# Loading two tokens per partition in 512-byte packets for the first chunk of a retention + GELU kernel, with its A, y and S products on smaller TensorE tiles

One core of one Trainium2 chip. The metric is the device time of one execution in microseconds (us); smaller is better. Runs are told fast or slow by their time and granted clock; only fast runs are compared: ratios are of fast runs alone, while medians are of all four runs of a kernel and say where one of them was slow.

## The reference, cut to what matters

```python
# q, k, v: [4 batches, 8 heads, 768 tokens, 64], float32
gamma = 1 - 2 ** (-5 - arange(8))                    # a decay per head
for t in range(768):
    state = gamma * state + einsum('bhd,bhe->bhde', k[:, :, t], v[:, :, t])
    y[:, :, t] = 1/8 * einsum('bhd,bhde->bhe', q[:, :, t], state)
x = y as rows [3072, 512]                            # token rows, heads side by side
out = gelu_tanh(x @ w_in) @ w_out                    # w_in [512, 2048], w_out [2048, 512]
```

The kernel works in six chunks of 128 tokens. Within a chunk it forms A = k qᵀ per head, multiplies by a decay mask, takes y = vᵀ A plus the part from the state, and updates the state with S = kᵀ v. Then come the two dense products. Chunk 0 has no state yet, so it needs q, k and v of its 128 tokens only, and it is the one chunk with nothing else to hide behind.

## The kernel before

Loads of chunk 0. A tile holds one token per partition, all 8 heads side by side; a head's token is 64 floats, so every packet has 256 bytes. One transfer per tile, over 128 partitions:

```python
def load1(eng, nm, c, b):
    eng.dma_start(out=ld_tile(nm, c, b),             # [128, 8, 64] float32
                  in_=srcs[nm][b, :, c*C:(c+1)*C, :].rearrange("h p d -> p h d"))
...
load1(nc.scalar, "q", 0, 0); load1(nc.sync, "k", 0, 0); load1(nc.scalar, "k", 0, 1)   # ... 12 tiles
```

A and y of a pair of heads, and the rows that leave:

```python
for hp in range(4):
    for j in range(2):                               # A: 64 rows x 128 columns, K = 64
        nc.tensor.matmul(out=ps[j][:, hp], lhsT=t[j*64:(j+1)*64, 1, hp], rhs=t[j*64:(j+1)*64, 0, hp], ...)
...
rows = out[b*S + c*C : b*S + (c+1)*C, :]             # 128 rows of 2048 bytes, one transfer
```

The order of GpSimd (POOL) in the opening; it issues the w_in and w_out loads, with a cast from float32, and prepares k:

```python
prep1(PO, "k", 0, 1)
nc.gpsimd.tensor_copy(out=misc[0:1, 4:5], in_=ld_tile("k", 0, 2)[0:1, 0, 0:1])   # waits for k of batch 2
load_w_in(0); load_w_in(1)
prep1(PO, "k", 0, 2); prep1(PO, "k", 0, 3)
for i in range(2, 5): load_w_in(i)
for i in range(4): load_w_out(i)
```

In program order TensorE takes for each batch the transposes of q and k, A, y; between them `spin(n)`, n dummy matmuls that are meant to keep its clock up. Then the first w_in products on half the tokens, S of each batch, the other half. After that the full 512-column products of w_in begin with "fc 4".

## Time and profile before

| | before |
|---|---|
| time, median (lowest to highest), 4 runs | 212.49 us (211.91 to 213.19) |
| span of the profiled execution | 210.3 us |
| TensorE (PE) busy, granted clock | 97%, 0.997 |
| start of fc 4 on the TensorE timeline (called F) | 21.03 us |
| from F to the end | 189.2 us |
| loads of chunk 0: transfers, rate from 4 to 11 us | 12, 288 GB/s |
| last load issued / first w_in issued / first w_in packet | 7.61 / 8.73 / 13.16 us |

(The prediction takes F from the chain of waits, which gives 21.19 to the same event.) F comes from one execution; the fast executions of the kernel before have spans from 210.2 to 212.8 us, so a difference in F of less than about 1 us is not read.

```profile
64.34 1.40 SPq L642 DMA_DIRECT2D out_dram<-o_sb  x3
65.79 4.28 SPq L98 DMA_DIRECT2D v<-in_v_dram  x4
```

In the first, w_in is issued and k of batches 2 and 3 prepared right after. In the second, three output tiles of chunk 0 leave on the SP queue in 1.4 us of issue, and the loads of v for chunk 2 follow without delay.

### The profile page before, as it was taken

To read this page: it belongs to the slowest core of one execution; us is meant where nothing else is said; L and a number is where in the kernel's file an instruction comes from. 1 tells how busy PE (TensorE), PEld (TensorE's weight loads), DVE (VectorE), ACT (ScalarE), POOL (GpSimd) and SP (SyncE) were. 2 spreads that over 40 slices of the span, in tenths; PEclk is the share of its full clock that TensorE was granted. 3 is DMA by queue.
4 is the path that set the end of the run, shared out by engine and by line. 5 is a ranking of instruction groups with operands and counts; after the bars stand their busy time and mean duration, and the time that the engine had idled before them with its cause. 6 is when DMAs were issued, how large, how long until landed. Compare 5 with 4: busy or idle time off the path is not lost.

```text
span 210.3 us, 3858 instructions
## 1 busy us (share of the span) xinstructions
PE 203.5 (97%) x1502; PEld 110.3 (52%) x1502; DVE 91.4 (43%) x162; ACT 84.3 (40%) x141; POOL 100.0 (48%) x121
## 2 busy tenths in 40 slices
PE   7789999999999999999999999999999999999993
PEld 2448444457897456444465444456444455444462
DVE  6678100298634757351847522647550652100001
ACT  2465661245465122565113566113466113565120
POOL 3596400433366867663787939651697611100000
PEclk9999999999999999999999999999999999999998
DMA  7999999997879989969988889897897021100112
GB/s 158 288 251 206 207 203 224 225 248 135 148 109 233 243 175 226 179 107 183 237 146 225 167 155 253 165 198 161 161 242 171 10 94 50 53 0 0 50 71 79
DMA packets 132738, 33.83 MB, mean 161 GB/s; under 512 B 126512, under 2 KB 130864, under 8 KB 132720
## 3 DMA queue, kind: packets, MB, share of 16 engines
q1 hardware_dynamic: 117328, 21.80, 53.3%
q0 software_dynamic: 5600, 8.65, 17.4%
q10 hardware_dynamic: 9792, 3.15, 6.2%
q8 instruction: 11, 0.18, 0.3%
q14 instruction: 7, 0.06, 0.1%
HBM read 31.48 MB, written 6.29 MB: 180 GB/s over the span
## 4 chain that ended last, share of the span: by engine, by line
PE 92%; DMA 3%; POOL 1%; ACT 1%; SPq 1%; DVE 0%; issue 0%
PE o_ps L469 40%; PE h_ps L424 40%; PE y_ps L299 3%; DMA k<-in_k_dram 3%; PE a_ps L264 3%; PE y_ps L286 2%; PE s_ps L318 2%; PE qkT_ps L239 1%; POOL w_in L408 1%; PE spin_ps L171 1%; POOL k L195 1%; SPq L98 1%; ACT qkT L224 0%; ACT v L190 0%; DVE o_sb L507 0%
## 5 line engine op out<-in xcount | busy, mean ns | idle before, releaser
L469 PE MATMUL o_ps<-w_out,g 128*128 128x512 f16 (+1 forms) x400 | 88.6, 371 | 0.0
L424 PE MATMUL h_ps<-xT,w_in 128*128 128x512 f16 (+1 forms) x464 | 85.6, 342 | 0.0
L439 ACT ACTIVATE g<-h_ps 128x512 f16<-128x512 f32 x96 | 57.3, 597 | 46.9 <-PE h_ps L424 46.8
L424 PEld LDWEIGHTS <-w_in 128*128 128x128 f16 x464 | 44.8, 98 | 37.4
L469 PEld LDWEIGHTS <-g 128*128 128x128 f16 x400 | 37.4, 98 | 38.6
L277 DVE TENSOR_TENSOR a_sb<-a_ps,mask 128x512 f16<-128x512 f32 x48 | 30.2, 684 | 17.9 <-PE a_ps L264 17.8
L491 ACT COPY o_sb<-o_ps 128x512 f32<-128x512 f32 x19 | 11.1, 586 | 51.5 <-PE o_ps L469 49.7
L195 POOL TENSOR_TENSOR k<-k,cst 128x512 f16<-128x512 f32 x23 | 23.9, 1061 | 12.5 <-DMA k<-in_k_dram 12.4
L344 POOL TENSOR_TENSOR stg<-st,cst 128x512 f32<-128x512 f16 x16 | 16.4, 1039 | 12.6 <-DVE st L335 10.7
L206 POOL TENSOR_TENSOR kT<-kT,cst 128x512 f16<-128x512 f32 x16 | 16.3, 1050 | 10.7 <-DMA kT<-in_k_dram 10.2
L496 POOL DMA_DIRECT2D out_dram<-o_sb x17 | 9.5, 562 | 23.0 <-ACT o_sb L491 16.1
L254 DVE STREAM_TRANSPOSE qkT<-q 128x512 f16<-128x512 f16 x16 | 11.4, 712 | 13.8 <-POOL q L206 13.8
L206 POOL TENSOR_TENSOR q<-q,cst 128x512 f16<-128x512 f32 x16 | 16.3, 1050 | 1.8 <-PE h_ps L424 1.8
L254 DVE STREAM_TRANSPOSE qkT<-kT 128x512 f16<-128x512 f16 x16 | 10.9, 698 | 13.3 <-POOL kT L206 13.3
L335 DVE TENSOR_TENSOR st<-s_ps,stg 64x256 f16<-64x256 f32 x32 | 13.5, 422 | 5.0 <-PE s_ps L318 4.4
L195 DVE TENSOR_TENSOR q<-q,cst 128x512 f16<-128x512 f32 x8 | 6.1, 757 | 16.5 <-DMA q<-in_q_dram 16.5
L226 DVE CAST xT<-y_ps 128x512 f16<-128x512 f32 x11 | 7.2, 687 | 12.7 <-PE y_ps L299 12.7
L192 POOL CAST v<-v 128x512 f16<-128x512 f32 x16 | 9.6, 616 | 6.3 <-DMA v<-in_v_dram 5.2
L507 DVE COPY o_sb<-o_ps 128x256 f32<-128x256 f32 x2 | 0.8, 424 | 26.6 <-PE o_ps L469 26.6
L224 ACT CAST xT<-y_ps 128x512 f16<-128x512 f32 x13 | 7.2, 587 | 11.8 <-PE y_ps L299 11.8
L171 PE MATMUL spin_ps<-zero 128*128 128x512 f16 x30 | 8.9, 437 | 1.3 <-DVE zero L139 1.3
L264 PE MATMUL a_ps<-qkT 64*128 64x128 f16 x192 | 8.1, 218 | 1.3 <-ACT qkT L224 1.3
(34 smaller groups left out, 88.2 us busy)
## 6 DMA issues: line engine op xcount, KB each, us to landing
v<-in_v_dram SPq DMA_DIRECT2D x22, 256.0 KB, 4.3
k<-in_k_dram SPq DMA_DIRECT2D x20, 256.0 KB, 4.4
out_dram<-o_sb POOLq DMA_DIRECT2D x17, 256.0 KB, 3.0
q<-in_q_dram SPq DMA_DIRECT2D x64, 64.0 KB, 2.8
kT<-in_k_dram SPq DMA_DIRECT2D x64, 64.0 KB, 2.8
w_out<-in_moe_w_out_dram POOLq DMA_DIRECT2D x4, 512.0 KB, 16.1
w_in<-in_moe_w_in_dram POOLq DMA_DIRECT2D x3, 512.0 KB, 9.4
q<-in_q_dram SPq DMA_DIRECT2D x5, 256.0 KB, 5.9
```

The lines of the kernel that those rows point to most:

```text
L171: nc.tensor.matmul(out=ps, lhsT=zero[:, 0:128], rhs=zero, start=True, stop=True)
L195: eng.tensor_tensor(out=t, in0=src, in1=cst[:, col:col + H].unsqueeze(2).broadcast_to([128, H, Dh]), op=ALU.mult,)
L206: nc.gpsimd.tensor_tensor(out=t, in0=ld_all((key, c))[:, b * NHP:(b + 1) * NHP].rearrange("p hp a d -> p (hp a) d"), in1=cst[:, col:col + ...
L254: nc.vector.transpose(out=qkT_tile(c, b)[:, "qk".index(nm)].rearrange("p hp t -> p (hp t)"), in_=blk16.pop((nm, c, b)).rearrange("p ha d - ...
L264: nc.tensor.matmul(out=ps[j][:, hp], lhsT=t[j * 64:(j + 1) * 64, 1, hp], rhs=t[j * 64:(j + 1) * 64, 0, hp], start=True, stop=True,)
L277: nc.vector.tensor_tensor(out=s, in0=ps[j], in1=mask[:, j], op=ALU.mult)
L335: eng.tensor_tensor(out=st[sl, :, b, sl], in0=s_ps[sl, :, sl], in1=stg[sl, :, b, sl], op=ALU.add,)
L344: nc.gpsimd.tensor_tensor(out=stg[:, :, b], in0=st[:, :, b], in1=cst[:, OG:OG + NHP].unsqueeze(2).broadcast_to([128, NHP, 128]), op=ALU.mult,)
L424: nc.tensor.matmul(out=out, lhsT=w_in_of(fc, kc), rhs=xT[c][:, kc, t0:t1], start=(kc == 0 and first), stop=(kc == NHP - 1), skip_group_che ...
L439: nc.scalar.activation(out=out, in_=in_, func=AF.Gelu_apprx_tanh, scale=1.0)
L469: nc.tensor.matmul(out=ps[:, n0:n1], lhsT=g_sb[c, fc // 2][:, fc % 2, b * C:(b + 1) * C], rhs=w_out_sb[fc // (NF // NO)][:, fc % (NF // NO ...
L491: nc.scalar.copy(out=o_sb, in_=ps)
```

## The change

Its intent: 512-byte packets for the loads of chunk 0, as the DMA engines are full there with 256-byte ones. A partition takes tokens 2t and 2t+1 of a head; heads 0 to 3 lie on partitions 0 to 63, heads 4 to 7 on 64 to 127. Hence two transfers of 64 partitions per tile, 64x64 tiles for A and y, 64-row tiles for S, masks for permuted tokens, and permuted output rows. The order of work in chunk 0 was changed with it. The core of the diff:

```diff
+    def load_pair(eng, nm, b):
+        for hh in range(2):
+            eng.dma_start(
+                out=ld_tile(nm, 0, b)[hh*64:(hh+1)*64].rearrange("p (mi e) d -> p mi (e d)", e=2),
+                in_=srcs[nm][b, hh*4:(hh+1)*4, 0:C, :].rearrange("mi (tp e) d -> tp mi (e d)", e=2))
     def load1(eng, nm, c, b):
+        if c == 0:
+            load_pair(eng, nm, b)
+            return
# ... masks: eight memsets and one select become six selects on 64 partitions; the old mask is made later
     def mm_A(c, b):
+        if c == 0:
+            for n in range(16):
+                m, e, i, hh = n >> 3, n >> 2 & 1, n >> 1 & 1, n & 1
+                nc.tensor.matmul(out=ps[i][hh*64:(hh+1)*64, 2*m+e],
+                                 lhsT=t[i*64:(i+1)*64, 1, 2*hh+m, e*64:(e+1)*64],
+                                 rhs=t[i*64:(i+1)*64, 0, 2*hh+m], ...)
# ... likewise y (16 matmuls, two banks) and S (8 per batch on two row tiles, two banks, four copies)
     def ev_O(c, b):
         rows = out[b*S + c*C : b*S + (c+1)*C, :]
+        if c == 0:
+            rows = rows.rearrange("(t e) n -> e t n", e=2)
# ... order in chunk 0, POOL:
     prep1(PO, "k", 0, 1)
     (wait for k of batch 2)
     load_w_in(0)
+    prep1(PO, "k", 0, 2)
     load_w_in(1)
-    prep1(PO, "k", 0, 2)
     prep1(PO, "k", 0, 3)
# ... v of batch 2 loaded by SP instead of ACT; first qkT copy on DVE instead of ACT; y before the next A; 18 spins in place of 16 after the first 14 (cut)
```

More of the change, by code (lines that the diff above doesn't have):

```diff
@@ L50 @@
     kdec_t = g_t ** (160.0 - t_t)
-    cst_np = np.concatenate([qdec, kdec, gst, qdec_t, kdec_t], axis=1).astype(np.float32)
+    hh_p, tp_p = np.arange(128)[:, None] // 64, np.arange(128)[:, None] % 64
+    mi_c, e_c = np.arange(8)[None, :] // 2, np.arange(8)[None, :] % 2
+    g_p, t_p2 = gam[4 * hh_p + mi_c], 2.0 * tp_p + e_c
+    qdec_p = g_p ** (t_p2 - 32.0) * 0.125
+    kdec_p = g_p ** (160.0 - t_p2)
+    ig_p = 1.0 / g128[4 * hh_p + np.arange(8)[None, :] // 2 % 2 * 2 + np.arange(8)[None, :] // 4]
+    ig = np.tile(1.0 / np.concatenate([g128[0::2], g128[1::2]]), (128, 1))
+    cst_np = np.concatenate(
+        [qdec, kdec, gst, qdec_t, kdec_t, qdec_p, kdec_p, ig_p, ig], axis=1
+    ).astype(np.float32)
     cst_h = nc.inline_tensor(cst_np, name="rr_cst")
@@ L64 @@
     OQ, OK, OG, OQT, OKT = 0, H, 2 * H, 2 * H + NHP, 2 * H + NHP + 16
+    OQP, OKP, OIP, OI, NCST = OKT + 16, OKT + 24, OKT + 32, OKT + 40, OKT + 48
     misc = const.tile([128, 32], F32)
-    cst = const.tile([128, 64], F32)
+    cst = const.tile([128, 128], F32)
     iden = const.tile([128, 128], F16)
@@ L95, in ld_tile @@
         return raw[nm, c, b]
+    def load_pair(eng, nm, b):
+        for hh in range(2):
+            eng.dma_start(
+                out=ld_tile(nm, 0, b)[hh * 64:(hh + 1) * 64].rearrange(
+                    "p (mi e) d -> p mi (e d)", e=2
+                ),
+                in_=srcs[nm][b, hh * 4:(hh + 1) * 4, 0:C, :].rearrange(
+                    "mi (tp e) d -> tp mi (e d)", e=2
+                ),
+            )
     def load1(eng, nm, c, b):
+        if c == 0:
+            load_pair(eng, nm, b)
+            return
         eng.dma_start(
@@ L124, in hold @@
         nc.gpsimd.tensor_copy(out=ld_tile(nm, c, b)[0:1, 0, 0:1], in_=until)
-    nc.sync.dma_start(out=cst[:, :OKT + 16], in_=cst_h.ap())
+    nc.sync.dma_start(out=cst[:, :NCST], in_=cst_h.ap())
     load1(nc.scalar, "q", 0, 0)
@@ L134 @@
     load1(nc.sync, "q", 0, 3)
+    load1(nc.sync, "v", 0, 2)
     load1(nc.sync, "v", 0, 3)
@@ L139 @@
     nc.vector.memset(zero, 0.0)
-    mask = const.tile([128, 2, NHP, 128], F32, name="mask")
     nc.vector.memset(iden, 1.0)
-    for j in range(2):
-        for hp in range(NHP):
-            nc.vector.memset(mask[:, j, hp], float(1.0 / g128[2 * hp + j]))
     nc.gpsimd.affine_select(
@@ L154, with make_mask @@
     )
-    nc.gpsimd.affine_select(
-        out=mask.rearrange("p j hp t -> p (j hp) t"),
-        in_=mask.rearrange("p j hp t -> p (j hp) t"),
-        pattern=[[0, 2 * NHP], [1, 128]],
-        base=0,
-        channel_multiplier=-1,
-        compare_op=ALU.is_ge,
-        fill=0.0,
-    )
+    mask_p = const.tile([128, 2, 4, 128], F32, name="mask_p")
+    for hh in range(2):
+        sl = slice(hh * 64, (hh + 1) * 64)
+        for f, e0, de in ((1, 0, 1), (0, 0, 2), (0, 1, 2)):
+            n = 8 // de
+            nc.gpsimd.affine_select(
+                out=mask_p[sl].rearrange("p i s (f t) -> p (i s) f t", f=2)[:, e0::de, f],
+                in_=cst[sl, OIP + e0:OIP + 8:de].unsqueeze(2).broadcast_to([64, n, 64]),
+                pattern=[[0, n], [1, 64]],
+                base=-e0,
+                channel_multiplier=-1,
+                compare_op=ALU.is_ge,
+                fill=0.0,
+            )
+    mask = const.tile([128, 2, NHP, 128], F32, name="mask")
+    def make_mask():
+        nc.gpsimd.affine_select(
+            out=mask.rearrange("p j hp t -> p (j hp) t"),
+            in_=cst[:, OI:OI + H].unsqueeze(2).broadcast_to([128, H, 128]),
+            pattern=[[0, H], [1, 128]],
+            base=0,
+            channel_multiplier=-1,
+            compare_op=ALU.is_ge,
+            fill=0.0,
+        )
     nc.scalar.activation(
@@ L193, in prep1 @@
         else:
-            col = OQ if nm == "q" else OK
+            col = (OQP, OKP, OQ, OK)[(nm == "k") + 2 * (c > 0)]
+            if c == 0:
+                dst = t.rearrange("p (e mi) d -> p mi e d", e=2)
+                src = src.rearrange("p (mi e) d -> p mi e d", e=2)
+                dec = cst[:, col:col + H].rearrange("p (mi e) -> p mi e", e=2)
+                dec = dec.unsqueeze(3).broadcast_to([128, 4, 2, Dh])
+            else:
+                dst, dec = t, cst[:, col:col + H].unsqueeze(2).broadcast_to([128, H, Dh])
             eng.tensor_tensor(
-                out=t,
+                out=dst,
                 in0=src,
-                in1=cst[:, col:col + H].unsqueeze(2).broadcast_to([128, H, Dh]),
+                in1=dec,
                 op=ALU.mult,
@@ L236, in mm_T @@
         ps = bank("att", F16, (128, 2, NHP, 128), "qkT_ps")
-        for i, nm in enumerate("qk"):
+        for i, nm in enumerate("qk") if c == 0 else ():
+            src = h16[nm, c, b].rearrange("p (e m i) d -> p m e (i d)", m=2, e=2)
+            dst = ps[:, i].rearrange("p (hh m) (e t) -> p m e hh t", m=2, e=2)
+            for m in range(2):
+                for e in range(2):
+                    nc.tensor.transpose(out=dst[:, m, e], in_=src[:, m, e], identity=iden)
+        for i, nm in enumerate("qk") if c > 0 else ():
             for hp in range(NHP):
@@ L261, in mm_A @@
         ps = [bank("att", name=f"a_ps{j}") for j in range(2)]
+        pss["A", c, b] = ps
+        if c == 0:
+            for n in range(16):
+                m, e, i, hh = n >> 3, n >> 2 & 1, n >> 1 & 1, n & 1
+                nc.tensor.matmul(
+                    out=ps[i][hh * 64:(hh + 1) * 64, 2 * m + e],
+                    lhsT=t[i * 64:(i + 1) * 64, 1, 2 * hh + m, e * 64:(e + 1) * 64],
+                    rhs=t[i * 64:(i + 1) * 64, 0, 2 * hh + m],
+                    start=True,
+                    stop=True,
+                    skip_group_check=True,
+                )
+            return
         for hp in range(NHP):
@@ L270, in mm_A @@
                 )
-        pss["A", c, b] = ps
     def ev_A(c, b):
@@ L276, in ev_A @@
             s = att.tile([128, NHP, 128], F16, tag=f"a{j}", name=f"a_sb{j}")
-            nc.vector.tensor_tensor(out=s, in0=ps[j], in1=mask[:, j], op=ALU.mult)
+            nc.vector.tensor_tensor(out=s, in0=ps[j], in1=(mask if c else mask_p)[:, j], op=ALU.mult)
             a_sb[c, b, j] = s
     def mm_yc(c, b, tag):
+        if c == 0:
+            pss["Y", c, b] = [bank(tag, name=f"y_ps{hh}") for hh in range(2)]
+            return
         y_ps = pss["Y", c, b] = bank(tag, name="y_ps")
-        if c == 0:
-            return
         for hp in range(NHP):
@@ L296, in mm_yi @@
         y_ps = pss["Y", c, b]
+        for n in range(16) if c == 0 else ():
+            m, e, i, hh = n >> 3, n >> 2 & 1, n >> 1 & 1, n & 1
+            sl = slice(hh * 64, (hh + 1) * 64)
+            nc.tensor.matmul(
+                out=y_ps[hh][i * 64:(i + 1) * 64, m],
+                lhsT=h16["v", c, b][sl, 4 * m + 2 * i + e],
+                rhs=a_sb[c, b, i][sl, 2 * m + e],
+                start=(e == 0),
+                stop=(e == 1),
+                skip_group_check=True,
+            )
+        if c == 0:
+            return
         for hp in range(NHP):
@@ L302, in mm_yi @@
                     rhs=a_sb[c, b, j][:, hp],
-                    start=(c == 0),
+                    start=False,
                     stop=True,
@@ L310, in ev_Y @@
             xT[c] = xp.tile([128, NHP, B * C], F16, tag="x", name="xT")
-        copy_on(eng, xT[c][:, :, b * C:(b + 1) * C], pss.pop(("Y", c, b)))
+        y_ps = pss.pop(("Y", c, b))
+        if c == 0:
+            for hh in range(2):
+                copy_on(
+                    eng[hh] if isinstance(eng, tuple) else eng,
+                    xT[c][:, 2 * hh:2 * hh + 2, b * C:(b + 1) * C],
+                    y_ps[hh][:, 0:2],
+                )
+            return
+        copy_on(eng, xT[c][:, :, b * C:(b + 1) * C], y_ps)
     def mm_s(c, b, tag="att"):
         if c + 1 >= NCk:
+            return
+        if c == 0:
+            s_ps = pss["S", c, b] = [bank(tag, name=f"s_ps{hh}") for hh in range(2)]
+            k_ = h16["k", c, b].rearrange("p (e m i) d -> p m e (i d)", m=2, e=2)
+            v_ = h16["v", c, b].rearrange("p (m i e) d -> p m e i d", m=2, e=2)
+            for n in range(8):
+                m, e, hh = n >> 2, n >> 1 & 1, n & 1
+                sl = slice(hh * 64, (hh + 1) * 64)
+                nc.tensor.matmul(
+                    out=s_ps[hh][:, m],
+                    lhsT=k_[sl, m, e],
+                    rhs=v_[sl, m, e],
+                    start=(e == 0),
+                    stop=(e == 1),
+                    skip_group_check=True,
+                )
             return
@@ L332, in ev_S @@
             if c == 0:
-                copy_on(eng, st[sl, :, b, sl], s_ps[sl, :, sl])
+                for hh in range(2):
+                    copy_on(
+                        eng, st[sl, 2 * hh:2 * hh + 2, b, sl], s_ps[hh][sl, 0:2, sl]
+                    )
             else:
@@ L487, in ev_O @@
         o_sb = op.tile([128, d_model], F32, tag="o", name="o_sb")
+        if c == 0:
+            rows = rows.rearrange("(t e) n -> e t n", e=2)
         if b == B - 1 and c > 0:
@@ L525 @@
     mm_T(0, 0)
-    ev_T(0, 0, AC)
-    load1(AC, "v", 0, 2)
     prep1(VE, "q", 0, 1)
+    ev_T(0, 0)
+    prep1(AC, "v", 0, 0)
     prep1(PO, "k", 0, 1)
@@ L540 @@
         load_w_out(i)
+    make_mask()
     spin(4)
@@ L545 @@
     ev_T(0, 1, AC)
-    prep1(AC, "v", 0, 0)
     prep1(VE, "q", 0, 2)
     spin(3)
-    mm_A(0, 1)
-    ev_A(0, 1)
     mm_yc(0, 0, "o")
@@ L553 @@
     ev_Y(0, 0, AC)
+    mm_A(0, 1)
+    ev_A(0, 1)
+    mm_T(0, 2)
+    ev_T(0, 2, AC)
     prep1(AC, "v", 0, 1)
-    mm_T(0, 2)
-    ev_T(0, 2)
-    spin(3)
+    prep1(VE, "q", 0, 3)
+    spin(5)
     mm_yc(0, 1, "o")
@@ L561 @@
     mm_A(0, 2)
-    prep1(VE, "q", 0, 3)
     ev_A(0, 2)
-    spin(2)
     mm_T(0, 3)
     ev_T(0, 3, AC)
+    prep1(AC, "v", 0, 2)
+    prep1(AC, "v", 0, 3)
     spin(4)
@@ L569 @@
     ev_A(0, 3)
-    prep1(AC, "v", 0, 2)
-    prep1(AC, "v", 0, 3)
+    spin(2)
+    t01, t23 = (0, half), (half, 2 * half)
+    m1a = [moe1_parts(0, fp, *t01) for fp in range(2)]
+    m1a[0](range(2))
+    m1a[1](range(2))
     mm_yc(0, 2, "o")
@@ L574 @@
     ev_Y(0, 2, AC)
-    t01, t23 = (0, half), (half, 2 * half)
-    m1a = [moe1_parts(0, fp, *t01) for fp in range(2)]
-    m1a[0](range(2))
-    mm_s(0, 0)
-    m1a[1](range(2))
+    m1a[0](range(2, 4))
+    m1a[1](range(2, 4))
     mm_yc(0, 3, "o")
@@ L584 @@
     ev_Y(0, 3)
-    m1a[0](range(2, 4))
+    mm_s(0, 0)
+    ev_S(0, 0)
     mm_s(0, 1)
-    m1a[1](range(2, 4))
+    ev_S(0, 1)
     for b in range(2):
-        ev_S(0, b)
         moe1_two(0, b, *t23, "oh"[b])
-        mm_s(0, 2 + b)
+    mm_s(0, 2)
     ev_S(0, 2)
+    mm_s(0, 3)
     ev_S(0, 3)
```

## The prediction

> **What bounds the kernel now.** I read the page first, then the chain that ended last in order of time, then the timeline of the first 22 us. Engine shares come first:
>
> ```profile
> PE 203.5 (97%) x1502; PEld 110.3 (52%) x1502; DVE 91.4 (43%) x162; ACT 84.3 (40%) x141; POOL 100.0 (48%) x121
> PE 92%; DMA 3%; POOL 1%; ACT 1%; SPq 1%; DVE 0%; issue 0%
> ```
>
> TensorE is 97% busy and 92% of the last chain. The change touches chunk 0 of six only, so I ask where in the span the chain is not TensorE. From the chain in order of time:
>
> ```profile
> 2.36 6.18 DMA k<-in_k_dram
> 8.78 1.60 POOL w_in L408 x2
> 10.38 1.08 POOL k L195
> ...
> 14.25 1.01 ACT qkT L224
> 15.26 0.53 ACT v L190
> 15.84 0.41 PE y_ps L299 x8
> ...
> 20.97 0.22 PE s_ps L318 x4
> 21.19 10.36 PE h_ps L424 x48
> 31.55 9.50 PE o_ps L469 x44
> ```
>
> Until 15.8 us the chain runs through loads, POOL, ACT; from there it is TensorE without a gap, and from 21.19 us (the first full 512-column product of w_in, "fc 4") TensorE has the same work in both kernels to the end at about 207 us. So the change is worth what it does to **the moment at which fc 4 starts**; I call it F, and F = 21.19 us now. The loads of that opening:
>
> ```profile
> 4.00:6.00 2.00, 2.00 (x13) 0.95 (x12) 1.38 (x2) 0.57 (x2) 0.00 (x0) 1.00 1.27 287
> 10.00:12.00 2.00, 1.46 (x26) 0.90 (x21) 1.67 (x4) 1.40 (x3) 2.00 (x3) 1.00 1.28 289
> 16.00:18.00 2.00, 2.00 (x31) 1.51 (x28) 1.20 (x3) 0.88 (x2) 1.63 (x3) 1.00 1.26 210
> ```
>
> In these stretches (columns: PE, PEld, DVE, ACT, POOL busy, clock, DMA share, GB/s) the DMA engines are full. 12 tiles of 256 KB land 0.9 us apart at 288 GB/s, q of batch 0 at 3.99 us, v of batch 3 at 14.4; then w_in follows. In the landings behind the timeline, the w_in part that fc 4 needs is complete at 20.07, only 1.1 us before F. Last, the steps of one batch:
>
> ```profile
> 6.88 0.78 DVE L195 TENSOR_TENSOR q<-q,cst 128x512 f16<-128x512 f32 x1 [1.04 <-DMA q<-in_q_dram]
> 8.28 1.29 DVE L277 TENSOR_TENSOR a_sb<-a_ps,mask 128x512 f16<-128x512 f32 x2 [0.62 <-PE a_ps L264]
> 8.76 1.01 ACT L224 COPY qkT<-qkT_ps 128x1024 f16<-128x1024 f16 x1 [1.04 <-PE qkT_ps L239]
> 15.32 0.40 PE L264 MATMUL a_ps<-qkT 64*128 64x128 f16 x8 [0.24 <-ACT qkT L224]
> 17.84 0.69 DVE L226 CAST xT<-y_ps 128x512 f16<-128x512 f32 x1 [0.80 <-PE y_ps L299]
> 18.45 3.66 DVE L226 CAST st<-s_ps 64x256 f16<-64x256 f32 x8
> ```
>
> Per batch: prepare q and k, transpose, copy (about 1 us on ACT, 0.69 on DVE), A, mask (1.29), y, copy (0.59 ACT, 0.69 DVE). These latencies, not the size of the matmuls, are the opening.
>
> **What the Trainium skill says.** (1) "DMA: Bandwidth & Descriptors", section "Why small descriptors are slow (HBM only)": a fixed overhead of about 3 cycles per packet. The trace agrees: dividing 16 engines by packet counts in full stretches, an engine starts a packet every 9.6 ns at 128 B, 14.1 at 256 B, 78.4 at 2048 B: 5 ns plus 36 ns per KB. (2) "SBUF — State Buffer", section "Door 1": a transfer to partitions 0 to 63 reaches 8 of 16 ports and was measured there at 196 GB/s. (3) The same page, "Can I just issue two DMAs to hit both halves?": two transfers to the two halves gained only 6%. No load of the kernel before goes to 64 partitions, so its trace neither confirms nor denies (2) and (3). (4) "TensorEngine Tiling (Array Packing)", "Key Properties": different tiles run in parallel, and a mode switch drains. The trace agrees on the first: the eight A matmuls start in pairs 3 ns apart, a pair every 56 ns.
>
> **The change part by part.**
> *Loads.* 512-byte packets: from the line above 5 + 18 = 23.2 ns, 353 GB/s, a tile in 0.74 us instead of 0.91 (estimate), all twelve 1.97 us sooner. That would move the w_in landing from 20.07 to 18.1: a floor for F, so the whole change can gain at most **3.1 us (1.5%)**. But each tile is now two DMAs of 64 partitions. Both queues begin with the lower half; while both write the same half I expect some 217 GB/s (8 ports at 27.2, the skill's figure), in opposite halves up to 353. Half and half gives 2/(1/217 + 1/353) = 269 GB/s, no better than 288. I take a rate about as before to 20% better: q of batch 1 (fourth tile, 6.85 us before) at 6.2 to 7.0.
> *TensorE.* A and y take 16 matmuls in place of 8, four in parallel: 4 groups x 56 ns + 220 ns = 0.4 us, as before. S takes 8 on two row tiles: as before. Zero, plus perhaps 0.1 us for drains.
> *Evictions.* y is split over two banks: by a fit of 587 ns at 512 and 1010 ns at 1024 columns ACT needs 0.38 us per half, 0.77 for 0.59: +0.18 per batch. DVE (687 ns at 512, 424 at 256): 0.85 for 0.69. S: four 64x128 copies a batch at about 0.29 us, 1.17 for 0.84; mm_s of batch 3 now needs the two banks that S of batch 1 holds.
> *Masks.* Eight DVE memsets (1.15 us) go, but DVE then waits for q at 4.0 us: free. POOL gets six selects on 64 partitions, 2048 columns a partition in place of 1024: some 2.4 us, behind the constants that land at 2.8, so k of batch 1 is prepared from about 5.4, as its load lands. The later mask (1.1 us of POOL after the w_out issues) is beside other work.
> *Order.* The copy of the first transposes goes from ACT (1.01) to DVE (0.69), but behind the preparation of q of batch 1, so it waits for that landing.
>
> Sum, with 353 GB/s: q1 lands 6.2, prepared 7.0, qkT 7.7 (7.72 before), A 8.15, masked 9.55 (9.57 before). y of batch 0 10.0, its copy on ACT to 10.8; transposes of batch 2 copied by ACT 10.85 to 11.85 (0.8 earlier than before, as k2 is prepared between the two w_in issues); v1 on ACT to 12.5; y1 12.95; its copy to 13.8; qkT of batch 3 13.8 to 14.8 (15.26 before). A3 at 14.85, **0.47 sooner**. Then, in TensorE's order: A 0.23, two spins 0.43, w_in products 0.87, y2 0.34, products 0.87, y3 0.4: 18.0. DVE copies y3 to 18.9, S0 to 20.1, S1 to 21.25; TensorE runs the two pairs of w_in products 18.95 to 20.7 and S2, then waits for S1's banks: S3 ends and **F = 21.5**. Before, from A3 to F took 5.87 us; now 6.65: two spins ahead of the products, 0.4 for the wait for y3, 0.3 for S banks. The gain at A3 is given back. At 269 GB/s, q1 lands at 7.0 and all of it comes 0.8 later: F = 22.3. Weighing both, F = 21.5 to 21.9, or +0.3 to +0.7 us.
>
> **The rivals.** *A: the loads dominate and the port limit does not bite.* For it: DMA full from 3 to 34 us, and the chain's 6.18 us in a load of k. Against it: the chain above is held after 8 us by ACT and DVE in turn. If the packets ran at 420 GB/s (the best 2048-byte stretch in the trace was 418), q1 lands 0.6 sooner, F = 20.9, and 212.4 us; with shorter drains and copies than I count, F = 19.5, 211 us.
> *B: the half-partition loads are slower than before.* For it: the skill's 196 GB/s and both queues starting in the same half. At 217 throughout, 12 tiles take 14.5 us instead of 10.9; q3 would land 3 us late at 15, and F = 24: 215.5 us. Against it: two queues, which drift apart.
> *C: a new wait on software-queue loads.* The first packet of w_in came at 13.16, 4.4 us after its issue, just as the ACT queue ran dry. With v2 moved off that queue it runs dry sooner, and w_in mixes with q3, v2 and v3. They could land late; they have 1 to 3 us of slack. Worth within 0.5 us either way.
>
> **Range and chances.** Before is 212.75. My sum gives +0.3 to +0.7; that the order and the spins were visibly re-tuned for this version argues for rival A, so I put the centre at +0.1: 212.9. A at its best and B half-way give 211.0 to 214.8. Faster by 2% needs F at 16.9, below the floor of 18.1 that w_in sets: 0.02. Slower by 2% needs B in full: 0.04. Within 2%: 0.94.
>
> **What would show it.** Right: packets of 512 B in the DMA view; GB/s of 270 to 350 in the opening; A and y groups of 16 in about 0.4 us; fc 4 starting at 21 to 22 us; DVE's S copies or the copy of y3 as what ends TensorE's waits just before it; everything after it unchanged. Wrong: over 380 GB/s, or under 230, in the opening; A groups at 0.6 us; w_in landing as what releases fc 4; or a difference that arises after 25 us.

## More of the kernel before

POOL's timeline (start us, duration us, engine, line, operation), and that of the SP queue, which issues most loads:

```profile
8.73 1.65 POOL L408 DMA_DIRECT2D w_in<-in_moe_w_in_dram  x2
10.38 2.07 POOL L195 TENSOR_TENSOR k<-k,cst 128x512 f16<-128x512 f32 x2
```

## The result

| | before | changed |
|---|---|---|
| time, median (lowest to highest), 4 runs each | 212.49 us (211.91 to 213.19) | 234.37 us (232.59 to 237.43; one run slow) |
| span, granted clock | 210.3 us, 0.997 | 230.9 us, 0.96 |
| F | 21.03 us | 29.43 us (+8.4) |
| from F to the end | 189.2 us | 201.4 us (+12.2) |

The ratio of fast runs is 1.100, 95% interval 1.0915 to 1.1086. (A ratio is the mean time of one kernel's fast runs over that of the other's of the same rounds, so not quite the ratio of the medians.) The prediction, 211.0 to 214.8, was far out. The loss has two parts, 8.4 us before F and 12.2 us after, where nothing was expected.

The page of the changed kernel, engine shares, and shares of the last chain:

```profile
PE 211.5 (92%) x1584; PEld 112.6 (49%) x1584; DVE 90.7 (39%) x163; ACT 84.2 (36%) x144; POOL 102.8 (45%) x127
...
PE 78%; DMA 10%; SPq 7%; POOL 2%; ACTq 1%; DVE 0%; ACT 0%; issue 0%; POOLq 0%
```

TensorE's share of the chain fell from 92% to 78%, and the SP queue, 1% before, has 7%. The chain in order of time (start us, duration us, what) tells where:

```profile
10.55 7.08 DMA k<-in_k_dram
...
17.78 1.04 POOL k L247
...
29.50 10.47 PE h_ps L538 x48
...
75.36 2.00 SPq L760
77.41 4.97 SPq L126
82.44 4.98 SPq L126
87.52 3.11 SPq L126
```

**Before F.** The second half of k of batch 3 took 7.08 us from issue to landing, and everything waited. POOL's timeline (in brackets: idle before, and what ended it):

```profile
10.20 1.03 POOL L247 TENSOR_TENSOR k<-k,cst 128x512 f16<-128x512 f32 x1 [0.39 <-DMA k<-in_k_dram]
...
17.78 1.03 POOL L247 TENSOR_TENSOR k<-k,cst 128x512 f16<-128x512 f32 x1 [5.81 <-DMA k<-in_k_dram]
18.77 2.30 POOL L522 DMA_DIRECT2D w_in<-in_moe_w_in_dram  x3
```

POOL waits for that k until 17.78, and as its queue is in order, the rest of w_in is issued at 18.77 in place of 12.37. What TensorE waited for is k:

```profile
18.87 0.61 PE L295 MATMUL qkT_ps<-iden,k 128*128 128x128 f16 x4 [1.88 <-POOL k L247]
```

It did not wait for w_in afterwards: the third part, the last that fc 4 needs, landed at 24.17 us, 5.3 us before F. From 16 to 18 us TensorE was busy for 0.44 us only, and its clock was then low. The stretches view (PE, PEld, DVE, ACT, POOL busy, clock, DMA share, GB/s):

```profile
18.00:20.00 2.00, 1.13 (x6) 0.71 (x7) 0.00 (x0) 0.48 (x1) 2.00 (x3) 0.50 0.26 69
20.00:22.00 2.00, 2.00 (x20) 0.68 (x19) 0.20 (x1) 1.57 (x3) 2.00 (x4) 0.50 0.61 98
```

The granted clock is 0.50 here (from 17.95 to 24.78 us); in the same stretches of the kernel before it was 1.00. From 18 to 20 us the DMA share is 0.26 too, where full stretches of these kernels read 1.14 to 1.28.

So the 8.4 us are made up as follows. A of batch 3 starts at 21.12 us in place of 15.32: 5.8. From there to F takes 8.31 us in place of 5.71, without a wait of TensorE: with the new order and tiles it is 6.65 at full clock (e1 and e12 below), so 0.9 is theirs, and the other 1.7 goes with the low clock.

**After F.** The SP queue's timeline:

```profile
72.31 5.06 SPq L760 DMA_DIRECT2D out_dram<-o_sb  x3
77.41 14.12 SPq L126 DMA_DIRECT2D v<-in_v_dram  x4
```

Set beside 64.34 and 65.79 of the kernel before: the issue of the same four loads of v takes 14.1 us, not 4.3. The DMA view from 76 to 92 us (40 slices of 0.4 us; busy tenths, then GB/s):

```profile
DMA  1211111111111111128981111111114795111159
GB/s 31 61 41 51 51 51 51 51 51 51 46 51 51 51 51 51 51 77 211 276 205 60 51 51 51 51 51 51 51 51 137 196 297 147 52 46 36 36 127 218
```

For most of that time about a tenth of the engines' time is used, at 51 GB/s. The trace's landing events say which transfers these are: an ordinary transfer raises its semaphore 16 times; each of the three output transfers of chunk 0 on this queue has 3 events, one 0.4 us after its issue ends, and the last at 80.5, 85.6 and 90.7 us: one every 5.1 us, 256 KB / 5.1 us = 51 GB/s. They run two engines wide. The Trainium skill explains it in a place that the prediction did not use: "DMA: Bandwidth & Descriptors", section "Why a DMA increments its semaphore by 16 and not by 1": the number of engines is the largest one up to 16 that divides the slowest dimension (not of size 1) of both sides, and the sequencer adds the missing increments itself. The rows had become [2, 64, 512], so 2. The fourth output tile leaves on POOL's software queue. It has 16 landing events, but the last comes 9.0 us after issue in place of 3.1, and while it is under way SP already takes 13.4 us to issue 16 loads of k in place of 9.2.

### The profile page after: what moved, and what is told of

Its sections match the earlier page's. It is cut to its first block, busy times and chain, and to the rows that moved or that the text cites. A ratio compares the mean times of both kernels' runs of the same rounds, so it can differ in the third digit from the quotient of the medians.

```text
span 230.9 us, 4052 instructions
## 1 busy us (share of the span) xinstructions
PE 211.5 (92%) x1584; PEld 112.6 (49%) x1584; DVE 90.7 (39%) x163; ACT 84.2 (36%) x144; POOL 102.8 (45%) x127
## 4 chain that ended last, share of the span: by engine, by line
PE 78%; DMA 10%; SPq 7%; POOL 2%; ACTq 1%; DVE 0%; ACT 0%; issue 0%; POOLq 0%
PE h_ps L538 36%; PE o_ps L583 31%; SPq L126 6%; DMA k<-in_k_dram 5%; DMA v<-in_v_dram 3%; PE a_ps L336 2%; PE y_ps L385 2%; DMA q<-in_q_dram 2%; PE s_ps L429 2%; PE y_ps L359 2%; PE spin_ps L215 1%; POOL k L247 1%; POOL kT L258 1%; SPq L760 1%; PE qkT_ps L298 1%; ACTq L113 1%
## 5 line engine op out<-in xcount | busy, mean ns | idle before, releaser
L583 PE MATMUL o_ps<-w_out,g 128*128 128x512 f16 (+1 forms) x400 | 90.2, 375 | 0.0
L538 PEld LDWEIGHTS <-w_in 128*128 128x128 f16 x464 | 45.3, 99 | 38.6 <-issue 0.6
L348 DVE TENSOR_TENSOR a_sb<-a_ps,mask 128x512 f16<-128x512 f32 x40 | 25.0, 684 | 16.5 <-PE a_ps L336 16.3
L247 POOL TENSOR_TENSOR k<-k,cst 128x512 f16<-128x512 f32 x23 | 23.4, 1040 | 17.8 <-DMA k<-in_k_dram 17.8
L313 DVE STREAM_TRANSPOSE qkT<-q 128x512 f16<-128x512 f16 x16 | 11.4, 712 | 16.6 <-POOL q L258 16.6
L449 DVE TENSOR_TENSOR st<-s_ps,stg 64x256 f16<-64x256 f32 x32 | 13.5, 422 | 7.3 <-PE s_ps L429 6.8
L236 POOL CAST v<-v 128x512 f16<-128x512 f32 x16 | 9.4, 611 | 15.6 <-DMA v<-in_v_dram 15.6
L278 DVE CAST xT<-y_ps 128x512 f16<-128x512 f32 (+1 forms) x12 | 7.4, 643 | 22.3 <-PE y_ps L385 19.1
L313 DVE STREAM_TRANSPOSE qkT<-kT 128x512 f16<-128x512 f16 x16 | 10.9, 699 | 12.9 <-POOL kT L258 12.9
L276 ACT CAST xT<-y_ps 128x512 f16<-128x512 f32 (+1 forms) x16 | 7.5, 510 | 22.5 <-PE y_ps L385 18.5
L385 PE MATMUL y_ps<-a_sb,v 128*64 128x128 f16 x160 | 7.5, 240 | 5.9 <-POOL v L236 5.9
L215 PE MATMUL spin_ps<-zero 128*128 128x512 f16 x32 | 10.7, 482 | 1.3 <-DVE zero L168 1.3
## 6 DMA issues: line engine op xcount, KB each, us to landing
w_out<-in_moe_w_out_dram POOLq DMA_DIRECT2D x4, 512.0 KB, 14.4
```

What stands on the lines that cost most here:

```text
L215: nc.tensor.matmul(out=ps, lhsT=zero[:, 0:128], rhs=zero, start=True, stop=True)
L247: eng.tensor_tensor(out=dst, in0=src, in1=dec, op=ALU.mult,)
L313: nc.vector.transpose(out=qkT_tile(c, b)[:, "qk".index(nm)].rearrange("p hp t -> p (hp t)"), in_=blk16.pop((nm, c, b)).rearrange("p ha d - ...
L348: nc.vector.tensor_tensor(out=s, in0=ps[j], in1=(mask if c else mask_p)[:, j], op=ALU.mult)
L385: nc.tensor.matmul(out=y_ps[j * 64:(j + 1) * 64, hp], lhsT=h16["v", c, b][:, 2 * hp + j], rhs=a_sb[c, b, j][:, hp], start=False, stop=True ...
L449: eng.tensor_tensor(out=st[sl, :, b, sl], in0=s_ps[sl, :, sl], in1=stg[sl, :, b, sl], op=ALU.add,)
```

## The experiments

"F" is the start of fc 4 in the profiled execution. All had 3 rounds; times are medians of 4 runs, one of which was slow in e5, e10 and e11.

### 1. Output rows in two transfers (e1)

```diff
         if c == 0:
-            (one transfer: rows [2, 64, 512] <- o_sb [128, 512])
+            parts = [(rows[e], o_sb[e*64:(e+1)*64]) for e in range(2)]    # two transfers of 64 rows
```

> The changed kernel with one edit: each output tile of chunk 0 (128 rows in permuted order) leaves as two transfers of 64 rows, one for even and one for odd tokens, in place of one transfer whose rows are addressed as [2, 64, 512]. Theory R (the one transfer ran on 2 of the 16 DMA engines, as its 2 landings plus one in place of 16 and some 50 GB/s suggest, and the loads of chunk 2 queued behind it): the loss after 60 us goes, about 12 us, so 221 to 224 us, and the output transfers take about 3 us each with 16 landings. Rival theory S (the loss after 60 us is an echo of the late start, 8.3 us, which pushes all later loads back): no change, 232 to 236 us.

218.31 us (217.48 to 220.25), ratio to before 1.025 (1.020 to 1.031); correct. SP's timeline:

```profile
69.00 4.72 SPq L765 DMA_DIRECT2D out_dram<-o_sb  x6
73.77 3.22 SPq L126 DMA_DIRECT2D v<-in_v_dram  x4
```

The loads of v take 3.2 us of issue again, every output transfer has 16 landings, the last 2.5 to 4 us after issue, and from F to the end it is 188.9 us, as before the change. So theory R holds and S falls: the loss after F was the row addressing, all of it. The gain of some 16 us is more than the 12 expected; the profiled execution also has F at 26.93 in place of 29.43, though the two kernels are the same up to the output. k of batch 3 and the third part of w_in landed within 0.12 us of each other in the two. The clock was at 0.50 from 17.95 to 24.78 us in the changed kernel and from 14.35 to 17.76 in e1. Whether that difference is chance stays open.

### 2. The permuted rows alone, in the kernel before (e2)

```diff
+        if c == 0:
+            rows = rows.rearrange("(t e) n -> e t n", e=2)     # wrong order of rows on purpose
```

> The kernel before with only the row order of chunk 0's output changed to the [2, 64, 512] addressing in one transfer (wrong order of rows on purpose, same bytes). Theory R: slower by about 10 to 12 us, 222 to 225 us, with TensorE idle between 65 and 95 us and the opening unchanged (first full w_in product at 21.2 us). Theory S: as before, 212 to 213 us.

230.14 us (229.22 to 231.58), ratio 1.078 (1.074 to 1.082). F is 21.82. SP's timeline:

```profile
69.38 5.09 SPq L644 DMA_DIRECT2D out_dram<-o_sb  x3
74.52 14.11 SPq L98 DMA_DIRECT2D v<-in_v_dram  x4
```

One line of addressing costs 17 us. That is more than expected and more than the 12.2 in the changed kernel; there TensorE is already late, so that less of the queue's delay is left to wait for. The traces fit: the issue of the last v ends 18.6 us later than before here and 21.5 us later in the changed kernel; less the lateness of F (0.8 and 8.4) that is 17.8 and 13.1 us, and from F to the end 18.8 and 12.2 us more were measured. (No run of its own tests this.)

### 3 to 5. The shape of the loads, one property at a time (e3, e5, e4)

All three are the kernel before with only the loads of chunk 0 altered.

```diff
 # e3: two transfers of 64 partitions, 256-byte packets
+ for hh in range(2): dma(tile[hh*64:(hh+1)*64], src[b, :, hh*64:(hh+1)*64, :].rearrange("h p d -> p h d"))
 # e5: two transfers of 4 heads, 128 partitions, 256-byte packets
+ for hh in range(2): dma(tile[:, hh*4:(hh+1)*4], src[b, hh*4:(hh+1)*4, 0:C, :].rearrange("h p d -> p h d"))
 # e4: one transfer, 128 partitions, 512-byte packets (wrong tokens on purpose)
+ dma(tile as "p (mi e) d -> p mi (e d)", src[b, 0:4, 0:2*C, :].rearrange("mi (p e) d -> p mi (e d)", e=2))
```

> The kernel before with each load of chunk 0 as two transfers of 64 partitions, packets still 256 bytes, nothing else. Theory H (transfers to 64 partitions and twice as many of them feed slowly, and w_in gets in between): the opening loads fall under 260 GB/s, the last loads of chunk 0 land at 16 us or later, first full w_in product at 24 to 30 us, 216 to 221 us. Rival theory O (the opening is lost to the new order of work on the engines, not to the transfers): as before, within 1 us of 212.5.

> The kernel before with each load of chunk 0 as two transfers of 4 heads each over all 128 partitions, 256-byte packets. It has the same number of transfers as the split by partitions (e3, 220.5 us), but every transfer reaches all partitions. Theory N (the number of transfers matters: each takes an issue and one of the 8 completion semaphores, so a queue runs dry and w_in gets in among the loads): first packet of w_in near 11 us, last k of chunk 0 after 16 us, 217 to 221 us. Theory Q (what matters is that a transfer writes to 64 partitions only): loads at 280 GB/s or more, first packet of w_in near 13 us, 212 to 214 us.

> The kernel before with each load of chunk 0 as one transfer of 128 partitions in 512-byte packets (wrong tokens on purpose, same bytes). By the fit of 5 ns plus 36 ns per KB the loads should run at about 350 GB/s, the twelve tiles land about 2 us sooner, w_in 2 us sooner, first full w_in product 0.5 to 1.5 us sooner: 211 to 212 us. If 512-byte packets themselves are what goes wrong (rival theory P), the rate stays under 290 GB/s and the time is 213 us or more.

| loads of chunk 0 | transfers | rate, 4 to 11 us | last k lands | F | time | ratio (95%) |
|---|---|---|---|---|---|---|
| before: 128 partitions, 256 B | 12 | 288 GB/s | 11.3 us | 21.03 | 213.3 and 212.8 | 1 |
| e4: 128 partitions, 512 B | 12 | 340 | 12.2 | 21.35 | 213.22 | 1.001 (0.995 to 1.007) |
| e5: 128 partitions, 256 B, by heads | 24 | 284 | 15.4 | 23.98 | 215.38 | 1.012 (1.008 to 1.017) |
| e3: 64 partitions, 256 B | 24 | 263 | 18.9 | 27.36 | 220.48 | 1.033 (1.029 to 1.036) |
| changed: 64 partitions, 512 B | 24 | 254 | 17.6 | 29.43 | 234.37 | 1.100 |

The rates are from the stretches view, one line of e3, e5 and e4 each:

```profile
4.00:11.00 7.00, 3.73 (x21) 1.40 (x18) 2.15 (x3) 2.02 (x3) 3.36 (x5) 1.00 1.18 263
```

```profile
4.00:11.00 7.00, 4.30 (x29) 1.89 (x28) 2.13 (x3) 2.50 (x3) 4.12 (x5) 1.00 1.27 284
```

```profile
4.00:11.00 7.00, 6.18 (x57) 3.01 (x55) 4.68 (x7) 2.54 (x3) 3.12 (x5) 1.00 1.14 340
```

Three things follow. Larger packets do load faster (340 beside 288), yet they gain nothing: **the opening was not bound by the rate of the loads.** In e4 the loads have landed by 12.9 us in place of 14.4 and F does not move, where 0.5 to 1.5 us sooner was expected; theory P falls by the rate. Second, two transfers per tile cost by themselves (e5), at an undiminished rate. Theory N holds in part: w_in's first packet came at 10.9 us as it said, but the last k at 15.4 us is short of its 16, and the time of 215.4 us lies between its 217 and the 214 of theory Q. Third, halves of partitions cost more time (e3) and 7% of the mean rate (263 beside 284 of e5), though from 6 to 8 us e3 ran at 284 GB/s too. Theory H holds but for its rate of under 260, and O falls.

Why should 24 transfers land so much later than 12 at nearly the same rate? The landings, set against the issue of w_in, give a pattern. "Late" means issued after the first part of w_in:

| | w_in issued | first w_in packet | last load issued | loads issued late | their time to landing |
|---|---|---|---|---|---|
| before | 8.73 us | 13.16 us | 7.61 us | 0 of 12 | |
| e4 | 9.05 | 11.42 | 6.97 | 0 of 12 | |
| e5 | 8.15 | 10.90 | 10.98 | 6 of 24 | 3.6 to 7.9 us |
| e3 | 8.95 | 11.02 | 12.82 | 6 of 24 | 7.5 to 9.2 us |
| changed | 8.90 | 11.01 | 14.72 | 6 of 24 | 6.1 to 8.3 us |

Before, every load was in the queues ahead of w_in. With 24 transfers the last six are issued behind it. The trace shows what delays their issue: the loads of SP and ACT share eight completion semaphores, and from the ninth transfer on each waits for an earlier one to land. Eight transfers are now 1 MB in flight and not 2. In the changed kernel 10 of the 16 loads issued from 3.67 us on are issued 0.02 us after the landing that frees their semaphore. Eight transfers of 128 KB at 4.1 us each from issue to landing are 256 GB/s (an estimate from these numbers), and 254 were measured, at a DMA share of 0.94 beside 1.14 in e4. That fits larger packets with too little in flight to be faster; no run tests it with more semaphores. Besides, a transfer to 64 partitions mostly held its queue for 0.59 to 0.80 us, one of the same bytes over 128 partitions (e5) mostly 0.37 to 0.53. Two loads issued just before w_in were as slow (9.35 us for one issued at 8.78 in e3, 6.46 for one at 8.24 in the changed kernel); they too had not landed when w_in's packets began. Once w_in moves, a late load is served packet by packet beside it, and w_in's packets are larger (1024 bytes written, beside 256 or 512). The Trainium skill ("DMA: Bandwidth & Descriptors", section "Queues, rings and completion order") states a round robin between the queue rows of an engine, and the trace agrees: where w_out, on the same software queue, overlaps a single load in the kernel before, from 31 to 34 us, 464 of its packets start and 470 of the load's, so that the load with its 256-byte packets gets 0.12 MB / 3 us = 40 GB/s. In the late stretch itself it is less even: from 13 to 15 us of the changed kernel 200 and 220 packets of the two load queues start, and 149 of w_in's.

Late landings are not the whole loss in e5 and e3. There ACT issues loads and also makes the first copy of transposes (qkT), and in its program order that copy stands behind the issue of k of batch 3, which waits for a semaphore. ACT's timeline in e5, and the same copy in the kernel before:

```profile
8.26 1.27 ACTq L100 DMA_DIRECT2D k<-in_k_dram  x2
9.56 1.01 ACT L231 COPY qkT<-qkT_ps 128x1024 f16<-128x1024 f16 x1 [3.07 <-DMA q<-in_q_dram]
```

```profile
6.71 1.01 ACT L224 COPY qkT<-qkT_ps 128x1024 f16<-128x1024 f16 x1 [2.12 <-PE qkT_ps L239]
```

So A of batch 0 starts at 10.63 us in e5 in place of 7.78, 2.9 us late, and A of batch 3 is 2.8 us late: nearly all that e5 loses at F. In e3 A of batch 0 is 3.8 us late and A of batch 3 is 6.3 us late, so about 2.6 us come later, where TensorE waits 1.1 us for q and 0.6 us for k of batch 3 and its clock is at 0.50 from 11.4 to 14.8 us. The changed kernel makes this first copy on DVE, and e5 and e3 do not show what the late k costs there; e9 below does. (This is read from the traces; no run moves the loads off ACT.)

### 6 to 8. Holding w_in back (e6, e8, e9)

```diff
 # e6 = e1 with:                                       # e8 = e3 with the same hold
+    prep1(PO, "k", 0, 2); prep1(PO, "k", 0, 3)
+    (POOL waits for the last v of chunk 0), then all of w_in, w_out
 # e9 = e1 with:
+    prep1(PO, "k", 0, 2)
+    (POOL waits for the first half of q of batch 3)
+    load_w_in(0); load_w_in(1)
+    prep1(PO, "k", 0, 3), then the rest of w_in, w_out
```

> The changed kernel with its output rows split (as e1, 218.3 us) and w_in held on GpSimd until the last v of chunk 0 has landed, both k preparations ahead of it. Theory W (w_in gets in among the loads and takes the engines from them packet by packet; the late k then holds up the rest of w_in on GpSimd): the loads land by 14 to 15 us, the w_in part that fc 4 needs by 22 to 23, fc 4 at 22.5 to 24 us in place of 26.9, 213.5 to 215.5 us. If the loads are slow of themselves on 64 partitions, they land after 16.5 us without w_in as well, and the time stays at 217 us or more.

> The kernel before with the loads of chunk 0 in two halves of 64 partitions (as e3, 220.5 us) and w_in held until the last v has landed. Theory W: the last k lands by 13.5 us in place of 18.9, fc 4 at 22.5 to 24.5 us in place of 27.4, 214 to 216 us. If not W: no better than 219 us.

> The changed kernel with split output rows (as e1, 218.3 us), and on GpSimd: k of batch 2 prepared, then a wait for the first half of q of batch 3 (it landed at 12.7 us in e6), then the first two parts of w_in, k of batch 3, the other parts. So w_in is issued at about 12.7 to 13 us, after nearly all loads are issued (the last at 12.9 in e6), but before they have all landed. Theory L (a load issued after w_in takes 6 to 9 us, one issued before it about 4; that is what the late k of batch 3 comes from): k3 lands by 14.8 us, w_in's first packet follows at once with no idle gap, fc 4 at 23 to 24.5 us, 214 to 216 us. If the late k3 has another cause, it lands after 16.5 us and the time stays at 217 or more.

| | k of batch 3 lands | first w_in packet | F | time | ratio (95%) |
|---|---|---|---|---|---|
| e1, no such hold | 17.5 us | 11.36 us | 26.93 | 218.31 | 1.025 (1.020 to 1.031) |
| e6 | 14.7 | 18.32 | 30.41 | 221.69 | 1.041 (1.036 to 1.046) |
| e9 | 14.3 | 14.70 | 25.04 | 216.62 | 1.016 (1.009 to 1.022) |
| e3, no such hold | 18.9 | 11.02 | 27.36 | 220.48 | 1.033 (1.029 to 1.036) |
| e8 | 14.1 | 17.24 | 25.93 | 218.03 | 1.027 (1.022 to 1.032) |

In all three the late k comes about 3 to 5 us sooner (in e8 at 14.1, not the 13.5 expected; in e6 the last v at 16.0, not by 15), so w_in beside it is what made it late. The times of e6 and e8 missed their expectation, e6 badly. The hold was set too late: POOL issued w_in at 16.7 and 15.6 us, its first packet followed 1.6 us later, and TensorE then waited for w_in (2.7 us in e6, 0.7 in e8) and not for k; in e6 its clock fell to 0.5 as well. In e8, where k was in time, A of batch 3 was still 4.1 us late, and A of batch 0 3.7: the copy on ACT again. e9 puts the issue where nearly all loads are issued but not yet landed, and it is the best correct form of the change, though F at 25.04 is above the 24.5 and 216.62 us above the 216 that were expected. Its timeline:

```profile
12.98 1.66 POOL L522 DMA_DIRECT2D w_in<-in_moe_w_in_dram  x2
...
14.66 1.06 POOL L247 TENSOR_TENSOR k<-k,cst 128x512 f16<-128x512 f32 x1
```

POOL no longer stands still between them. k that comes 3.3 us sooner than in e1 moves A of batch 3 from 20.28 to 18.05 us: that is what the late k cost, together with the stretch at clock 0.50 that e1 has and e9 does not. Of the 4.0 us by which F is still later than in the kernel before, A of batch 3 makes 2.7 (18.05 beside 15.32), the new order and tiles from there to F 0.9 (6.65 beside 5.71), and w_in itself, whose second part lands at 20.45 us against 16.57, only 0.3 (6.99 beside 6.65).

### 9. All of w_in issued before the last k is prepared (e10)

```diff
 # e1 with:
-    prep1(PO, "k", 0, 3)      # between load_w_in(1) and load_w_in(2)
+    prep1(PO, "k", 0, 3)      # after the last load_w_out
```

> The changed kernel with split output rows (as e1) and k of batch 3 prepared on GpSimd only after all w_in and w_out parts are issued. Theory G (the remaining parts of w_in are issued at 18.7 us only because GpSimd waits for k3 first, while the DMA engines then stand idle from 18 to 21): the third part of w_in lands at 20.5 to 22 us instead of 24, k3 later still than 17.5 as more w_in is ahead of it, at 19 to 24 us; the two pull against each other, F at 25 to 28 us, 216 to 220 us. It would be under 215 only if k3 did not suffer.

220.39 us (219.51 to 223.84), ratio 1.030 (1.023 to 1.037), F 28.95. The third part of w_in lands at 22.96 us, 1.1 us sooner than in e1, but less so than expected; k of batch 3 lands at 17.98 and is prepared only at 18.43, as POOL is still issuing. The late v now lands at up to 23.9 us in place of 19.8. It is not an improvement: theory G's two effects pull against each other, as expected, though F, the time and the third part of w_in lie just above their ranges (25 to 28, 216 to 220 and 20.5 to 22 us) and k lands before its range (19 to 24). TensorE waited 2.5 us for k and not for w_in; it had not waited for w_in in e1 either, so w_in sooner had nothing to give.

### 10. The order alone (e7), and the rest of the change without the load shape (e12)

e7 is the kernel before with the changed kernel's order in chunk 0 (the cut part of the diff above). e12 is e1 with

```diff
-    for hh in range(2): (two transfers of 64 partitions)
+    dma(tile as "p (mi e) d -> p mi (e d)", src[b, 0:4, 0:2*C, :].rearrange("mi (tp e) d -> tp mi (e d)", e=2))
     # one transfer of 128 partitions, 512-byte packets; wrong tokens on purpose
```

> The kernel before with the changed kernel's order of work in chunk 0 alone (its loads, masks, matmuls and rows as before). By the prediction's sum the new order gives back at the w_in products and S what it gains at A of batch 3: within 1 us of the kernel before, 212 to 214 us. If the order is a part of the loss (theory O), 215 us or more.

> The changed kernel with split output rows (as e1, 218.3 us) and each load of chunk 0 as one transfer over all 128 partitions, packets still 512 bytes (wrong tokens on purpose, same bytes). Theory L: with 12 transfers all loads are issued before w_in, run at about 340 GB/s, the last lands by 13.5 us, and what is left of the change is its order and its small tiles: fc 4 at 21.5 to 23 us as in the run of the order alone (22.4), 212.5 to 214.5 us. If the permuted tiles, split banks or masks cost something of their own, fc 4 is at 24 us or later and the time 215.5 us or more.

e7: 213.57 us, ratio 1.004 (1.001 to 1.007), F 22.43. e12: 214.09 us, ratio 1.007 (1.001 to 1.013), F 23.24, 0.2 over the expected upper end. So the new order costs a little under 1 us of time, and tiles, masks and split banks little more; with the row fix and a one-transfer load (319 GB/s from 4 to 11 us, about 340 expected), nearly all of the loss is gone. TensorE's timeline in e12:

```profile
16.59 0.42 PE L320 MATMUL a_ps<-qkT 64*64 64x128 f16 x16 [0.24 <-ACT qkT L271]
...
19.67 0.42 PE L368 MATMUL y_ps<-a_sb,v 64*64 64x128 f16 x16
...
22.57 0.74 PE L413 MATMUL s_ps<-v,k 64*128 64x128 f16 x16
23.24 1.04 PE L533 MATMUL h_ps<-xT,w_in 128*128 128x512 f16 x4
```

Sixteen 64x64 matmuls take 0.42 us, as eight took 0.40 before. From A of batch 3 to F it is 23.24 - 16.59 = 6.65 us, as in e1 (26.93 - 20.28).

### 11. A small rearrangement of the kernel before (e11)

```diff
     load_w_in(0)
+    prep1(PO, "k", 0, 2)
     load_w_in(1)
-    prep1(PO, "k", 0, 2)
```

> The kernel before with one edit: k of batch 2 is prepared on GpSimd between the first two issues of w_in, not after both, so about 0.8 us sooner. All loads are issued before w_in in either. If the copies and preparations of each batch set the opening (as the run with 512-byte packets on 128 partitions says, which gained nothing), fc 4 starts 0 to 0.8 us sooner, 212.0 to 212.9 us beside 212.8; if the second part of w_in, now issued a microsecond later, comes late, it is slower by up to 0.5 us.

213.04 us, ratio 0.996 (0.990 to 1.003), F 21.57 (one run of four slow). F did not come sooner, and there is no gain beyond noise. No version beat the kernel before clearly.

### F and the rest, over all runs

Span of the profiled execution less F: before 189.2; e1 188.9, e5 189.4, e6 189.0, e7 189.2, e9 188.8, e10 188.8, e11 189.2, e12 189.0; e3 191.1, e8 190.0, e4 190.7; changed 201.4, e2 208.1. The two that keep the two-engine rows stand out, and the others stay near 189. In e3, e8 and e4, with 1 to 2 us more, TensorE has later waits of 1.6, 0.9 and 1.2 us in all (for gelu on ACT in e3 and e8, mostly; for transposes copied by DVE in e4), where the kernel before has none; what brings them about is not shown.

## Why the prediction was wrong, point by point

- **"from 21.19 us ... TensorE has the same work in both kernels to the end"**, so that the change would be worth what it does to F. The work is the same, but its inputs came late: the step failed because the part by part list had no entry for the output rows. Their new addressing cost 12.2 us after F (e1 gets them back, e2 shows them alone). A part of the diff of one line had been left out. The prediction's own list of signs of being wrong had "a difference that arises after 25 us", and it came.
- **Rival C, "They have 1 to 3 us of slack. Worth within 0.5 us either way."** This is the step that failed before F. The mixing was foreseen, for q3, v2 and v3; its size was not, nor that k of batch 3 would be among the late. A load issued behind w_in took 6 to 8 us to land in place of about 4, k of batch 3 came at 17.6 us where the sum had its transposes copied from 13.8 us, and TensorE waited for it: A of batch 3 at 21.12 us, not 14.85. With k some 3 us sooner it starts at 18.05 and 18.38 (e9, e6) beside 20.28 (e1). POOL, in order, also held back the rest of w_in to 18.77, but TensorE did not wait for that. The prediction blamed the ACT queue running dry; the landings fit better to which transfers had been issued first: in e5 both queues still had packets when w_in began.
- **"each tile is now two DMAs of 64 partitions"**, then only a rate of 269 GB/s was drawn from it. The rate was nearly right (254), but by luck: its working has the ports full, and the trace has the engines not full (share 0.94 beside 1.14), which fits too few transfers in flight. The number of transfers, with eight completion semaphores, was missed, and e5 shows that it matters at full rate.
- **512-byte packets at 353 GB/s**: on 128 partitions 340 were measured, near enough. (The 418 GB/s of rival A are no rate in the trace: they count w_in's packets as 2048 bytes, where the trace has 1024 bytes written and 204 to 210 GB/s.) Rival A's gain from it was wrong: e4 had the rate and gained nothing. The prediction's own sentence, that the latencies of a batch and not the loads are the opening, was right against rival A.
- **TensorE groups at 0.4 us**: right, 0.42. **From A of batch 3 to F 6.65 us**: right to the hundredth in e12 and e1, but by luck. The waits that it counts, 0.4 us for the copy of y3 and 0.3 for the banks of S, are not there: TensorE has no wait of over 0.2 us between the two, and the 5.87 us that it gives for the kernel before end at F of the chain (5.71 on the timeline). The gain at A that it should offset (14.85 us) did not come: 16.59 in e12, where q of batch 1 landed at 7.36 and not at 6.2 to 7.0; in the changed kernel it landed at 8.00.
- **The clock** was taken as 1.00 throughout. It fell to 0.50 for 6.8 us before F and again after the second stall (0.51 from 90 to 100 us). From A of batch 3 to F took 8.31 us with it and 6.65 without.
- **Rival B at 215.5 us** named the half-partition loads, which are a part of it (e3 beside e5), but "two queues, which drift apart" was set against it, and its working counted bandwidth alone.

## What to carry to other kernels

Read every rearranged access pattern on its DMA side: the size of its slowest dimension, and how many landing events the trace shows, told here how many engines carried it, and the narrow transfers also delayed what was queued behind them. When a change splits transfers, count them against the completion semaphores and look at what is issued last: here a small load issued behind the stream of w_in took 6 to 8 us in place of 4. Ask, too, what else the issuing engine has to do: a copy on ACT stood 2.9 us behind load issues. Before making loads faster, test with wrong data of the right shape whether a faster load moves the end at all.

## What the Trainium skill lacked or had wrong

- "DMA: Bandwidth & Descriptors" has the rule for the number of engines, and the runs agree (3 landing events for a slowest dimension of 2, 51 GB/s). It lacks what that does to other transfers of the queue: four loads behind three such transfers took 14.1 us to issue in place of 4.3, and the kernel lost 12 to 17 us.
- "SBUF — State Buffer", section "Can I just issue two DMAs to hit both halves?", says that two transfers to the two halves gain 6% over one; with the 196 GB/s for one half in the page's table that is about 208 GB/s (an estimate from the page). Here two queues that both alternate between the halves ran at 254 to 263 GB/s on average, and at 284 for 2 us of e3, so the measurement is higher. How much slower halves are than full transfers is not settled here: 263 beside 284 at 256 bytes with as many transfers (e3, e5), while 254 beside 340 at 512 bytes compares 24 transfers with 12.
- No page gives the time that issuing takes by shape: mostly 0.59 to 0.80 us for a 128 KB load to 64 partitions, 0.37 to 0.53 us for one over 128.
- No page states when a transfer of the software queue (from GpSimd) begins beside full hardware queues: its first packet came 4.4 us after issue in the kernel before and 2.1 us in the changed one, and 1.6 us with the queues empty (e6, e8).
